# A banded attention with a gated feed-forward network: two last products behind the values, and a new written-out order

## The chip, the cores and the metric

The kernel runs on one core of one Trainium2 chip. The core has TensorE (PE, with its own queue of weight loads, PEld), VectorE (DVE), ScalarE (ACT), GpSimd (POOL) and SyncE (SP), which here only issues DMAs. Each engine runs its own instructions in the order of the program; semaphores hold an instruction back until another engine or a DMA is ready. The metric is the device time in microseconds (us), median of the runs. The kernel before took 745.35 us (three runs, 744.77 to 746.07).

## The reference

```python
def _attn_ref(q_l, k_l, v_l, q_g, k_g, v_g):          # 8 batches, 8 heads, 512 local and 32 global rows, width 64
    k_all = np.concatenate([k_g, k_l], axis=2); v_all = np.concatenate([v_g, v_l], axis=2)
    out_g = np.matmul(sm(scale * np.matmul(q_g, k_all.transpose(0, 1, 3, 2))), v_all)
    s_ll = np.where(np.abs(pos[:, None] - pos[None, :]) <= 32, scale * np.matmul(q_l, k_l.transpose(0, 1, 3, 2)), -1e9)
    s_lg = scale * np.matmul(q_l, k_g.transpose(0, 1, 3, 2))
    out_l = np.matmul(sm(np.concatenate([s_lg, s_ll], axis=-1)), v_all)
    return np.concatenate([out_g, out_l], axis=2)

def _moe_ref(x, w1, w2, w3, w_out):                    # x: 4352 rows of 512; d_ff is 1024
    return ((x @ w1) * (x @ w2)) @ w3 @ w_out
```

`sm` is a softmax over the last axis. The attention's output, heads side by side, is x of the second function.

## The kernel before, in words

The work is cut into some 3200 steps, each a few instructions of one engine. `PLAN` is a list of words such as `2479P`: step number 2479, on PE (A is ACT, D is DVE, V is POOL, S is SP). The list is the program's order: `list_schedule` only goes through it, and asserts that each step comes behind the steps it depends on (the lists that `add` is given). The instructions' semaphore waits follow from which tiles they read and write, in that order.

Attention runs over 32 pairs of heads, m = 0 to 31 (four per batch). For a pair: `scores` (step sp_m, 64 short matmuls, L431), on DVE the row maxima and on ACT the exponentials, sum, normalisation, two transposes on DVE (L457, L460), eight copies called moves (L474) on ACT, DVE and POOL, then `values` (step av_m, L485 to L496, 84 short matmuls). Scores and values take turns in a PSUM ring of two buffers named "pu".

The feed-forward part runs on split numbers, high and low halves, three matmuls for one product. `first` and `second` serve batches 0 and 1. From batch 2 on, `batch_seven` computes the gate products in seven instead of eight block products. For batch b and output column j = 0 to 7 the step m_b_j_ph (`seven`, L876) has four phases: phases 0 to 2 are 12 matmuls of 256 columns, phase 3, called the last product here, is 6. Columns 2q and 2q+1 are a column pair; it runs beside attention pair m = 4b + 4 + q, that is the next batch's. The even column uses PSUM banks "a" and "b", the odd column a buffer of the ring "pu" (tiles named j). After the last product DVE makes the gate product g1 (L902), and only then may the next column pair, or the next scores, take the bank again. Other steps of a column: cc and c2 (copies on ACT), a0 and b1 (DVE, L894 and L892), b0 and g0 (POOL or DVE). `second` (second_k_i, L638 to L640, 6 matmuls of 512 columns) multiplies by the folded weights.

SP issues the weight loads wl_b_q_x (512 KB each, L806, x = A0, A1, C0, C1, D, B0, B1) into a ring of seven buffers; each load waits until the products of the weights seven places before it are done: B1 of column pair q+1 waits for the last product of the odd column, B0 for that of the even column, D for phase 2 of both.

Of the kernel before, what the change touches and what calls it, by code (L numbers as in the profile page):

```python
# [31 lines left out]
def r(ap):  # L32
# [120 lines left out]
    1004D 1013A 1014D 1016D 1006D 1005A 2050S 1008D 1015A 1017A 1007A 1018D 2112P 1077D 1010D 1019A 1011A 1009A 2051S
    1020D 1021D 1040A 2109P 2110P 2052S 2116A 1023D 2126A 2123P 2127A 1022D 425S 2117D 1029A 1028D 2053S 1027D 1026V
    1030A 1031A 2128D 2113P 1038S 2124P 1024A 2054S 1025A 2119D 1032P 2118D 1033A 2120D 2114P 2129D 2125P 2130D 2131D
    1034A 1036V 2121D 2133V 998V 2132D 2056S 2137P 1035D 2141A 2055S 2134D 1041P 1050D 1042D 2138P 1051A 2135P 1044D
    1046D 1043A 2148P 1045A 1052D 2057S 1054D 1047A 2187V 1056D 1053A 2136P 2058S 1055A 1048D 1049A 1057A 2189D 2142A
    1058D 1059D 1864S 1061D 2152A 2149P 2139P 1060D 1113S 2153A 1064A 1067D 1066A 1062A 1068D 426S 1069D 1076S 1063A
    2150P 1065D 1070P 2143D 2195A 2145D 2219A 2155D 960V 2197A 427S 2154D 1151S 1078A 2199A 2144D 1071A 2140P 2146V
    1072A 2156D 2220D 2157D 2198D 2147D 1866S 2159A 2224S 2167A 2200V 2151P 2158D 1079P 2160D 1073D 1189S 2221A 1115A  # L160
    2223S 2188V 1080D 2191V 2168V 2201A 1088D 1090D 2229S 2203A 1092D 1082D 2196V 1084D 1094D 1091A 1089A 2161P 1086D
    2162P 359P 2202D 2249P 2190D 299S 2217A 2226S 2163A 2171A 1083A 428S 1093A 2192V 2165D 2205A 2207A 2225S 2222V
    1085A 360D 2172D 366D 361A 2169P 2208V 1081A 362D 2194V 2170P 2175A 363D 2176D 2173P 367A 2193D 2230S 364S 2209A
    2174P 2228S 2211A 2260P 1095A 368D 1087A 1096D 2177P 2178P 2179A 2212V 302S 369D 2210V 2213A 2264A 2253A 2180D
    2181P 1097D 1098D 2206V 2204D 1116A 1114S 2164S 2218D 370S 1099D 1104A 2182P 2261P 2214D 1101V 1100A 2227S 1105D
    1102D 2215A 2265A 1107V 2250P 1106V 365S 371S 2254A 1103V 2255D 2262P 2216V 2231S 2267D 2251P 2256D 2263P 1108P
    2257D 2266D 2258D 1109A 2252P 2183D 2270D 1110A 2268D 2269D 1117P 2259D 1111D 2271A 1126D 1127A 1118D 1119A 1128D
    2275P 1120D 1129A 2279A 1121A 1130D 1131A 2286P 1122D 1153V 2290A 1132D 1124D 2232S 2276P 2233S 2287P 2272D 1123A
    2234S 1133A 2235S 1191D 1192V 1125A 1112V 1134D 2280A 2277P 1135D 1137D 1136D 2236S 1074V 2291A 2288P 2185A 2273P
    2166S 2293D 2289P 2292V 1145V 1144A 1143V 1141A 2237S 1152S 1227S 2294D 2238S 1139V 1140A 2243S 1142A 2240S 2282D  # L170
    2274P 2241S 2239S 1138V 2281V 2283D 2284V 2295V 1146P 2278P 2285D 2301P 1147A 1148A 1149D 1154V 2296D 1155P 1156D
    1157A 1158D 1159A 2242S 2244S 1164D 1165A 2297V 2298V 2312P 2316A 1160D 1162D 1161A 1166D 1168D 1169A 1167A 1170D
    1171A 1163A 1172D 2299P 2300P 2184S 429S 2186S 2245S 2313P 1190S 1173D 2305A 1228S 1229A 1230A 2302P 2246S 2247S
    1150V 2317A 2306A 2314P 2318V 430S 1174D 1175D 1181D 1179A 1178A 1180A 1183D 2303P 1176D 2248S 1177D 1182D 2308D
    1184P 2304P 2320D 2307D 2309D 2319D 2321D 2310D 2311D 2315P 1185A 2322D 1186A 2327P 2331A 1187D 2323V 2324V 2377V
    1193P 1202D 1194D 2338P 1196D 1198D 1203A 1195A 1204D 1188V 1197A 2328P 1199A 1206D 1265S 2325P 2326P 1208D 1205A
    1207A 1209A 1200D 1201A 2385A 2387A 2342A 1303S 1266S 2332A 1210D 2339P 1211D 1213D 2329P 2389A 1212D 2388V 2343A
    1219A 1221D 1218D 1220A 1215A 2340P 1217D 1341S 1216D 2344V 1214A 1222P 2335D 2333D 2336V 2346D 2347V 2334D 2349A
    2345D 2390D 2341P 2330P 2348D 2414S 1223A 1224A 1225D 2337D 2350V 2357A 1231P 2381V 2391A 2386V 2351P 2352P 2409A
    1232D 1240D 1234D 1241A 2358V 2413S 301S 1242D 1244D 1236D 1246D 431S 1238D 372P 2392D 2439P 2410V 2419S 2353A  # L180
    2378D 2361A 2415S 2380V 2355A 2416S 1247A 373D 2359P 2382D 1235A 374A 2362D 1239A 375D 376D 2360P 2363P 2418S 2407A
    1237A 2417S 2383V 1233A 2365V 2395A 377S 2364P 2411A 1243A 379D 2366D 2397A 380A 2393A 1245A 2412D 2420S 381D 1248D
    2396D 2369V 2384V 2399A 2450P 382D 2367P 2370D 2379V 2401A 1267A 2400D 2398D 2368P 2454A 2371P 2372P 1268V 2394D
    1249D 2402V 2403A 432S 2443A 2404V 1250D 1251D 1252V 2440P 2451P 383S 1255D 2444A 378S 1254A 384S 2422S 1256A 2445D
    2455A 2405A 1253A 2441P 1257D 2421S 1259A 1379S 2423S 2452P 2354S 2456V 2446D 2447D 2448V 1258A 1260P 1261A 2406D
    2408D 1305A 2457D 2442P 2453P 2449D 1262D 2465P 2458D 2460D 2373A 1269P 2459D 1306D 1263D 2375A 2476P 2461V 1270D
    1278D 2469A 2424S 2466P 1304S 1271A 1279A 1280D 1272D 2426S 2425S 2462V 1274D 1276D 1282D 1273A 2427S 1281A 1284D
    2480A 1285A 1283A 1275A 2428S 1277A 2463P 1286D 1287D 1289D 2477P 1343A 1344V 2481A 2464P 1288D 1294V 1293V 2478P
# [80 lines left out]
def band_attention_glu_kernel(  # L269
# [22 lines left out]
    NP = H // 2  # L292
    PB = 1
    NF = PB * H
    NH = B * H
# [900 lines left out]
    def batch_seven(b):  # L1196
# [53 lines left out]
        for q in range(4):  # L1250
            for y in range(2):
# [163 lines left out]
    for b in range(NS, B):  # L1415
        batch_seven(b)
# [84 lines left out]
```

## Time and profile before

| what | value |
|---|---|
| median of 3 runs | 745.35 us (744.77 to 746.07) |
| the profiled execution's own time | 749.62 us |
| its span, first to last instruction | 747.7 us |
| PE busy | 720.7 us, 96% of the span |
| PEld, DVE, ACT, POOL busy | 84%, 66%, 52%, 30% |
| mean granted clock of TensorE | 0.993 |
| DMA | 176.60 MB, mean 236 GB/s; q1 holds the kernel's transfers, q8 and q14 are marked "instruction" (70 of 16 KB on q8: 1.15 MB) |

The page cuts the span into 40 slices; PE is at 9 tenths or more in nearly all of them. With an engine that full, the stretches in which it is not busy, and those in which it runs at a lower clock, are what is to be read. A wait view gives who waited for whom; "issue" stands where the engine waited for nothing that the profile shows. Weight loads (PEld) start ahead of their matmuls, so an idle stretch is read most sharply there.

### The profile page before, as it was taken

The numbers are of one execution on the slowest core, as the hardware profiler recorded it, in microseconds if no ns is written. First come the engines' busy times: TensorE is split into PE (matmuls) and PEld (weight loads), VectorE is DVE, ScalarE is ACT, GpSimd is POOL, SyncE is SP. The second block draws the span as 40 slices with busy tenths as digits, with TensorE's granted clock in tenths as the row PEclk, the third lists the DMA queues.
The fourth block names the chain that finished last, engine by engine and source line by source line (L and its number), as shares of the span: only waits on it lengthen the run. The fifth ranks groups of instructions, "written<-read, shape, count | busy, mean of one in ns | idle before, by whom it ended". The sixth has DMA issues, their size and how long they took to land.

```text
span 747.7 us, 22460 instructions
## 1 busy us (share of the span) xinstructions
PE 720.7 (96%) x8944; PEld 626.6 (84%) x8944; DVE 491.9 (66%) x1461; ACT 390.5 (52%) x1164; POOL 223.5 (30%) x334
## 2 busy tenths in 40 slices
PE   8999999999999999999999988999999999999994
PEld 5345788989989998889998977889988899899894
DVE  5999998885767765876568555856678667324211
ACT  3659986675455644754455634474555446222111
POOL 4013422342243332342244222333154143122100
PEclk9999999999999999999999999999999999999998
DMA  9786686687867897767974856677876685486740
GB/s 334 260 296 237 219 228 192 184 252 197 252 182 237 265 321 280 274 190 267 351 265 128 288 197 214 240 237 255 280 287 201 226 308 180 166 304 205 259 161 28
DMA packets 109091, 176.60 MB, mean 236 GB/s; under 512 B 11292, under 2 KB 57660, under 8 KB 108988
## 3 DMA queue, kind: packets, MB, share of 16 engines
q1 hardware_dynamic: 108988, 175.18, 71.1%
q8 instruction: 70, 1.15, 0.6%
q14 instruction: 33, 0.27, 0.1%
HBM read 144.97 MB, written 30.15 MB: 234 GB/s over the span
## 4 chain that ended last, share of the span: by engine, by line
PE 82%; DVE 6%; ACT 5%; DMA 3%; issue 2%; SPq 1%; ACTq 0%; DVEq 0%
PE j L876 15%; PE ap L876 14%; PE acc L638 8%; PE acc L640 8%; PE acc L639 8%; PE s L431 4%; PE av L485 4%; PE bp L605 2%; PE ap L605 2%; PE bp L606 2%; PE ap L606 2%; PE bp L607 2%; PE ap L607 2%; PE bp L876 2%; PE av L494 2%
## 5 line engine op out<-in xcount | busy, mean ns | idle before, releaser
L442 ACT ACTIVATE P<-P,small 128x128 f32<-128x128 f32 x256 | 99.9, 392 | 38.0 <-DVE small L436 37.8
L436 DVE CUSTOM_DVE_ANT_0 P<-s,cs 128x128 f32<-128x128 f32 x256 | 58.7, 286 | 36.8 <-PE s L431 35.7
L640 PE MATMUL acc<-w34h,gl 128*128 128x512 f32 x192 | 75.6, 394 | 0.0
L639 PE MATMUL acc<-w34l,gh 128*128 128x512 f32 x192 | 75.4, 393 | 0.0
L638 PE MATMUL acc<-w34h,gh 128*128 128x512 f32 x192 | 75.3, 392 | 0.0
L474 ACT COPY PT<-TT 32x256 f32<-32x256 f32 (+1 forms) x138 | 53.8, 390 | 14.8 <-DVE TT L457 10.0
L442 ACT ACTIVATION_READ_ACCUMULATOR P<-P,small 128x1 f32 x256 | 48.2, 188 | 0.0
L474 POOL COPY PT<-TT 32x256 f32<-32x256 f32 (+1 forms) x38 | 15.7, 413 | 106.0 <-DVE TT L457 92.4
L751 PE MATMUL w<-wo,w3f 128*128 128x512 f32 x96 | 44.1, 604 | 1.9 <-DVE wo L664 1.9
L431 PE MATMUL s<-KT,qp 64*32 64x128 f32 x2048 | 37.7, 274 | 6.3 <-issue 6.3
L640 PEld LDWEIGHTS acc<-w34h,gl 128*128 128x128 f32 x192 | 36.1, 188 | 7.4
L638 PEld LDWEIGHTS acc<-w34h,gh 128*128 128x128 f32 x192 | 36.1, 188 | 6.9 <-issue 0.8
L639 PEld LDWEIGHTS acc<-w34l,gh 128*128 128x128 f32 x192 | 36.1, 188 | 6.3
L452 DVE TENSOR_TENSOR P<-P,sums 128x1024 f32<-128x1024 f32 x32 | 39.9, 1248 | 0.8
L457 DVE STREAM_TRANSPOSE TT<-P 128x1024 f32<-128x1024 f32 x32 | 39.2, 1224 | 0.4
L431 PEld LDWEIGHTS s<-KT,qp 64*32 64x32 f32 x2048 | 28.7, 105 | 12.7 <-issue 7.7
L605 PE MATMUL ap<-x,w12h 128*128 128x256 f32 x128 | 36.1, 282 | 1.5 <-ACT as__1417 L611 0.8
L751 PEld LDWEIGHTS w<-wo,w3f 128*128 128x128 f32 x96 | 17.3, 190 | 22.9 <-issue 16.1
L888 POOL TENSOR_TENSOR bt<-bt 128x256 f32<-128x256 f32 x26 | 21.5, 829 | 50.3 <-ACT bt L890 49.9
L605 PE MATMUL bp<-x,w12h 128*128 128x256 f32 x128 | 36.2, 283 | 0.0
L607 PE MATMUL ap<-x,w12l 128*128 128x256 f32 x128 | 35.6, 278 | 0.2 <-DVE w12l L413 0.2
L485 PEld LDWEIGHTS av<-PT,vr 64*64 64x64 f32 x1024 | 28.5, 132 | 8.5 <-issue 4.3
(469 smaller groups left out, 2062.5 us busy)
## 6 DMA issues: line engine op xcount, KB each, us to landing
raw_w<-in_w_t_dram SPq DMA_DIRECT2D x22, 512.0 KB, 6.0
kq<-in_kp_t_dram SPq DMA_DIRECT2D x32, 272.0 KB, 5.4
out_dram<-o_None SPq DMA_DIRECT2D x33, 256.0 KB, 5.1
qp<-in_q_t_dram SPq DMA_DIRECT2D x32, 256.0 KB, 5.1
vr<-in_v_t_dram SPq DMA_DIRECT2D x32, 256.0 KB, 5.4
wg<-dm SPq DMA_DIRECT2D x16, 512.0 KB, 6.4
ws_0A<-dm SPq DMA_DIRECT2D x12, 512.0 KB, 5.3
ws_0C<-dm SPq DMA_DIRECT2D x12, 512.0 KB, 5.9
```

The costliest lines, as they stand in the source:

```text
L431: nc.tensor.matmul(st[32 * a : 32 * a + 32, x, 128 * e : 128 * e + 128], q[r, 128 * e + 32 * a : 128 * e + 32 * a + 32], k[r, o : o + 128] ...
L436: nc.vector.tensor_tensor_reduce(Ps[m % 2][:, x, e], T["s", m][:, x, 128 * e : 128 * e + 128], masks[e], -0.125, 3.0e38, ALU.add, ALU.min, ...
L442: nc.scalar.activation(p, p, AF.Exp, bias=T["mn", n][:, e : e + 1], scale=-1.0, accum_out=T["sm", m][:, x, e : e + 1])
L474: (nc.scalar.copy if eng is nc.scalar else eng.tensor_copy)(dst, src)
L485: nc.tensor.matmul(av[c, y, 128 * k + 32 * s0 : 128 * k + 32 * s1], V[r, x, k], PT[r, s0:s1, x, k], start=(k == 0), stop=False, **go)
L605: nc.tensor.matmul(d, wh, x[:, 0, 0:w], start=(k == m % 2 == 0), stop=False, skip_group_check=True)
L607: nc.tensor.matmul(d, wl, x[:, 0, 0:w], start=False, stop=(k == 3), skip_group_check=True)
L638: nc.tensor.matmul(a, gh[:, m % 2, sl], wh[:, c], start=(m == 0), stop=False, **part)
L639: nc.tensor.matmul(a, gh[:, m % 2, sl], wl[:, c], start=False, stop=False, **part)
L640: nc.tensor.matmul(a, gl[:, m % 2, sl], wh[:, c], start=False, stop=(m in (5, 7)), **part)
L751: nc.tensor.matmul(T["w34", t], w3f_of(t, j), wo_of(j), start=(j == 0), stop=(j == 7))
L876: nc.tensor.matmul(d, w[:, n, wy, kt, :], v[:, xy, :], start=(start and kt == c == 0), stop=(kt == 1 and c == 2), skip_group_check=True)
```

## The change

One line of the dependence lists, and the words of `PLAN` from its 1109th on. The line is in `batch_seven`; it made the last product of an even column (y == 0) depend on the values of its attention pair, and now does so for both columns:

```diff
-                    mid = [("av", NP * b + NP + q)] if ph == 3 and y == 0 and NP * b + NP + q < NH // 2 - 1 else []
+                    mid = [("av", NP * b + NP + q)] if ph == 3 and NP * b + NP + q < NH // 2 - 1 else []
```

In `PLAN` the first 1108 words are the same (up to the moves of pair 11), and so are the 524 words from second_8_6 behind the scores of pair 24 to the normalisation of pair 29. In the rest the words stand in another order, and 185 steps are on another engine (51 from DVE to POOL, 46 back, 33 from ACT to DVE, 23 back, 19 from POOL to ACT, 13 back). No step is added or removed. Two lines of it around the scores of pair 22 (1307P; 1298P is av_21, 2479P m_4_3_3, 2468P m_4_2_3, 2433S and 2431S the loads wl_4_2_B1 and wl_4_2_D, 433S the load of pair 22's v):

```diff
-    2470A 1290A 1297A 2430S 1291A 2484D 2483D 2467P 1295D 1296A 1292D 2479P 1298P 2472D 2473D 2471D 2482V 2374S 1299A
-    2486D 2468P 2475D 2485V 2474V 1300A 2487V 1301D 1307P 2429S 1316D 1308D 2491P 1309A 1310D 2431S 433S 2433S 1312D
...
+    1298P 1299A 2484D 2482V 2485D 2479P 2433S 2431S 1300A 2474V 2486D 2468P 1301D 1307P 2487V 1308D 2488V 433S 2502P
```

What stands on PE between the values of a pair and the next scores, where it differs (PE's order, read out of the two lists):

```
             before                          after
av_15        m_2_6_3 m_2_7_3                 m_2_6_3 m_2_7_3 second_4_6              sp_16
av_16        m_3_0_3                         m_3_1_3 m_3_0_3                         sp_17
av_17        m_3_2_3 m_3_4_0                 m_3_3_3 m_3_2_3 m_3_4_0                 sp_18
av_21        m_4_2_3                         m_4_3_3 m_4_2_3                         sp_22
av_22        m_4_4_3                         m_4_5_3 m_4_4_3 second_8_3              sp_23
av_30        m_6_4_3                         m_6_4_2 m_6_5_3 m_6_4_3                 sp_31
```

The list now has both last products behind the values in all 19 column pairs that the line names; before, it had so in 14 (that of pair 15 among them), and in those of pairs 16, 17, 21, 22 and 30 one of the two stood ahead of the values. SP's order around the scores of pairs 21, 22 and 23 (parts of its list):

```
21 before  wl_4_1_C1 store_6_0 wl_4_1_D load_q2_22 wl_4_1_B1 wl_4_1_B0
   after   wl_4_1_C1 store_7_0 wl_4_1_B0 wl_4_1_D wl_4_1_B1 load_q2_24
22 before  wl_4_2_C0 wl_4_2_D load_v_22 wl_4_2_B1 wl_4_3_A1 wl_4_2_B0
   after   wl_4_2_C1 store_6_128 wl_4_2_B1 wl_4_2_D load_v_22 wl_4_2_B0
23 before  wl_4_3_C0 load_v_23 wl_4_3_D load_k2_26 load_q2_24
   after   wl_4_3_C0 wl_4_3_A0 load_k2_25 wl_4_3_C1 wl_5_0_A0
```

On DVE, column pair 4, 5 of batch 2: before, b1_2_5, a0_2_5, g0_2_5, g1_2_4, with a0_2_5 behind m_2_5_3 in the list; after, a0_2_5 ahead of the values, then b1_2_4, b1_2_5, g1_2_4, with g1_2_4 ahead of m_2_5_3. At the end the first of the two last half evictions (out_16_128_0) goes from ACT to DVE.

## Rows read from the trace of the kernel before

**Rows 1.** Windows view by stage; columns: stretch, length, busy time (count) of PE, PEld, DVE...
```profile
236.00:477.57 241.57, 232.06 (x3208) 211.38 (x3191) 162.14 (x501) 128.38 (x405) 80.38 (x118) 0.99 0.75 253
477.57:590.00 112.43, 111.23 (x1433) 99.49 (x1428) 80.02 (x263) 60.87 (x194) 36.66 (x54) 1.00 0.74 252
590.00:738.30 148.30, 147.52 (x1358) 136.52 (x1358) 57.56 (x148) 45.41 (x116) 34.33 (x50) 1.00 0.62 210
```

**Rows 2.** Waits of the weight-load queue (PEld), 236 to 477.5; total, times, longest.
```profile
PEld s L431 <- issue: 6.2, 3, 2.8
...
PEld j L876 <- DVE cc L894: 1.0, 1, 1.0
PEld s L431 <- ACT gh L410: 1.0, 1, 1.0
```

**Rows 3.** Timeline at pair 22's scores, 435 to 439 (start, length, count, idle before).
```profile
434.94 0.81 PEld L431 LDWEIGHTS s<-KT,qp 64*32 64x32 f32 x54
...
438.56 0.17 PEld L431 LDWEIGHTS s<-KT,qp 64*32 64x32 f32 x10 [2.82 <-issue]
```

**Rows 4.** Timeline of PEld at pair 23's scores, 456 to 460.
```profile
459.88 0.14 PEld L431 LDWEIGHTS s<-KT,qp 64*32 64x32 f32 x2 [2.60 <-issue]
```

**Rows 5.** Windows view from gap to gap, and of the run-up to the second gap.
```profile
420.69:438.55 17.86, 15.21 (x252) 13.92 (x252) 9.43 (x31) 7.47 (x26) 5.99 (x10) 1.00 0.73 253
438.55:459.87 21.32, 18.13 (x252) 16.66 (x252) 11.11 (x34) 7.77 (x27) 3.82 (x6) 0.92 0.72 239
...
432.36:435.70 3.34, 3.34 (x139) 3.17 (x132) 1.55 (x5) 0.70 (x2) 2.49 (x3) 1.00 1.01 361
454.10:457.25 3.15, 3.15 (x138) 2.98 (x132) 1.74 (x4) 0.21 (x1) 1.90 (x2) 1.00 1.01 358
```

**Rows 6.** DMA view, 432.4 to 436.1: queue, kind, packets, MB, share of engines.
```profile
q1 hardware_dynamic: 541, 1.27, 95.1%
q14 instruction: 1, 0.01, 0.5%
```

**Rows 7.** DMA view, 436.1 to 438.6.
```profile
q8 instruction: 1, 0.02, 2.4%
```

**Rows 8.** DMA view, 438.6 to 441, GB/s in 40 equal slices.
```profile
GB/s 0 0 0 0 0 0 0 0 0 0 0 0 0 0 0 0 0 0 0 0 0 273 0 0 0 0 0 0 0 0 0 0 0 0 0 0 0 0 0 0
```

**Rows 9.** Timeline of SP's DMA issues, 404 to 482.
```profile
430.53 0.53 SPq L806 DMA_DIRECT2D ws_2D<-dm  x1
431.11 0.59 SPq L393 DMA_DIRECT2D vr<-in_v_t_dram  x1
431.89 0.32 SPq L806 DMA_DIRECT2D ws_2B<-dm  x1
```

**Rows 10.** Windows view of the two stretches at the lower clock (last columns: PEclk, DMA).
```profile
439.70:443.12 3.42, 3.42 (x18) 3.42 (x17) 1.49 (x13) 2.38 (x12) 0.00 (x0) 0.50 0.02 5
460.18:463.60 3.42, 3.42 (x17) 3.39 (x17) 2.54 (x18) 2.79 (x13) 0.00 (x0) 0.50 0.03 10
```

**Rows 11.** Timeline, 288 to 300: the wait before the first product of column 6.
```profile
294.92 0.42 DVE L894 TENSOR_TENSOR cc<-j,cc 128x256 f32<-128x256 f32 x1 [3.23 <-PE j L876]
...
296.24 1.61 PE L876 MATMUL ap<-x,ws_3A 128*128 128x256 f32 x12 [1.36 <-issue]
```

**Rows 12.** Timeline of PE, 448 to 466: the last product of column 5.
```profile
452.66 0.97 PE L876 MATMUL j<-x,ws_2B 128*128 128x256 f32 x6 [0.85 <-DVE cc L894]
```

**Rows 13.** The chain in order of time: scores 13, a product, values 13.
```profile
264.41 1.09 PE s L431 x64
...
273.93 1.36 PE j L876 x12
275.29 0.98 PE av L485 x30
```

**Rows 14.** Timeline of VectorE, 416 to 440: pair 21 from scores to values.
```profile
421.67 0.29 DVE L436 CUSTOM_DVE_ANT_0 P<-s,cs 128x128 f32<-128x128 f32 x1
...
430.71 1.09 DVE L474 COPY PT<-TT 32x256 f32<-32x256 f32 x2
```

**Rows 15.** Timeline of PE, 355 to 360: a bank taken again at once.
```profile
357.88 1.63 PE L876 MATMUL ap<-x,ws_2A 128*128 128x256 f32 x12 [0.52 <-DVE G1l L902]
```

**Rows 16.** Timeline of the end, 734 to 748.
```profile
738.30 0.65 ACT L645 COPY o<-acc 128x256 f32<-128x256 f32 x2 [0.77 <-PE acc L640]
```

More of the change, by code (lines that the diff above doesn't have):

```diff
@@ L250 @@
[L250 removed]
+    913V 912D 914A 300S 911A 1846P 2031S 917D 1995D 1976D 1978S 349D 916A 354A 1822S 1831P 1832P 1839A 885V 848V 350D
+    355D 1840D 1983D 1820S 351S 1847A 1848D 1901S 1984V 1997V 2032S 1977S 1985A 1986D 297S 2033S 1988S 927P 352S 1841P
+    1842P 356D 357S 1855P 1853P 2034S 2035S 2007A 2008V 1996D 1849A 1854P 1856P 1987S 928D 930D 931A 929A 932D 933A
+    2028V 1998V 934D 935A 936D 938D 939A 1850V 1851P 1852P 940D 942D 919A 920A 921D 1999D 2009A 2029A 2001D 2010D 1989D
@@ new lines @@
+    967A 981A 969A 1075S 2045S 2083P 979A 970D 971A 972D 425S 973A 982D 983D 985D 2100A 2086P 2047S 2084P 984D 2090A
+    2097P 2101A 2048S 2087P 986A 988D 993D 990D 987D 989D 2093D 992A 991A 2098P 2104D 1993S 2102V 994P 2092D 2103D
+    1039V 2088P 2105V 995D 2099P 2095D 2106D 2091V 2094D 1002A 2111P 996A 997D 2050S 1003P 2051S 1004D 2107A 2049S
+    2115A 1012D 1014D 2057S 2108V 1038S 2122P 1016D 1018D 1006D 1013A 1008D 1015A 998V 1017A 1010D 1005A 2109P 2052S
+    1007A 2110P 2053S 1011A 1009A 1019A 1020D 2126A 2112P 1021D 2123P 2116A 2117V 960V 2054S 2127A 1023D 2113P 1022D
@@ new lines @@
+    1062A 2144D 1070P 2159A 2140P 299S 1071A 2160D 2151P 2147D 2219A 1072A 2200V 1073D 2161P 2189V 2158D 2221A 2191D
+    2196D 2188D 1079P 1088D 2201A 2203A 2162P 1080D 2229S 2167A 1115A 2217A 1081A 2224S 2202V 1090D 2249P 428S 1082D
+    1092D 1084D 2192V 1094D 1083A 2171A 2163A 1086D 2222D 359P 2165A 2168D 1085A 2220D 2230S 2190D 360D 2169P 2205A
+    2194V 361A 2207A 2172D 362D 2208V 363D 366D 2209A 2193V 1093A 2210D 364S 1087A 2170P 1089A 2175A 367A 2228S 2173P
+    2176D 2174P 368D 2179A 1095A 2164S 1114S 369D 1091A 1096D 2211A 2260P 2180D 2177P 2213A 1097D 1116A 2204V 2178P
@@ new lines @@
+    2264A 2215A 370S 2206D 2181P 2182P 2227S 365S 2253A 2261P 1099D 1098D 2265A 2214V 1103A 2212D 2183D 1106A 371S
+    2250P 2262P 1107A 1101D 2254A 2251P 1104A 1102V 922V 2267D 2268D 1100A 1105A 2255D 2232S 1108P 2218D 2216D 2231S
+    2263P 2256D 2266V 2257D 1109A 1110A 1112V 2252P 2270D 2259D 1117P 2275P 2258V 1111D 1126D 1118D 1128D 2269V 1127A
+    2286P 1120D 1129A 1121A 1122D 1124D 2279A 2276P 1125A 1119A 1074V 2290A 2233S 2287P 2185D 1130D 1132D 1131A 1123A
+    2271V 2234S 1153V 2272D 2280A 1133A 302S 2235S 2277P 1191D 1192V 2291A 1134D 1135D 1137D 1136D 2236S 2288P 2273P
@@ new lines @@
+    1357A 2517P 1348D 435S 1358D 2528P 1360D 1350D 2515P 2521A 1361A 1349A 2567V 1351A 1359A 1352D 1353A 2569V 1362D
+    2518P 1363D 2532A 1365D 2575A 2522A 1364D 1368D 1371D 2529P 1367D 2519P 1370D 2533A 1373D 303S 2523D 1369A 1366A
+    2530P 1372A 2577A 2579A 2604S 1374P 1493S 1375A 2606S 436S 2536D 2599A 2524D 2520P 2535D 2531P 2580V 2568D 2525D
+    2376S 2534V 1376D 2526V 2527D 2547A 1377D 2601A 2537V 2571D 2581A 2538D 2576D 2516P 2539A 2540D 1383P 1384D 304S
+    2541P 2578D 2542P 2600V 1392D 1386D 1394D 1396D 1388D 1398D 1390D 2573V 2548D 2607S 2582D 2572D 2543A 2545A 2605S
@@ new lines @@
+    1264V 385P 386D 2551V 2552D 387A 2570D 388D 2608S 2602V 2574V 389D 392D 1457A 1458A 2629P 2610S 1418S 2549P 2550P
+    2555V 2556D 393A 394D 390S 2585A 2587A 2588V 2583A 2584V 2589A 2590V 2586V 1395A 1397A 1385A 1393A 1389A 2553P
+    1302V 2554P 2557P 2558P 2609S 306S 2544S 395D 396S 391S 397S 1226V 2597A 2598V 2640P 2611S 2546S 305S 2633A 2630P
+    2612S 1391A 1387A 1399A 1400D 2644A 2641P 2559A 2560D 2561P 1401D 2562P 2591A 2593A 2594D 2592D 1402D 1403D 1409D
+    2645A 1410D 2642P 1405D 2634A 2635D 2613S 2631P 1406D 2595A 2646V 1419A 1456S 2614S 2637D 2636D 1408A 1407A 1411A
@@ new lines @@
+    2790V 2743P 407D 1539A 2791A 2744P 2830P 2792V 2745A 2760D 2746D 1549A 2764D 2775A 1646S 2777A 2779A 2749V 2781A
+    440S 2783A 1543A 2774V 2785A 1551A 2747P 408D 1572D 2778V 2787A 2750D 1537A 2748P 2784V 2834A 2782D 2751P 409S
+    1552D 2823A 2776D 2752P 2780D 1553D 1555D 2820P 2824A 2786V 1554D 1556D 1560D 2825D 404S 1559D 410S 2831P 1563A
+    2835A 1562V 1561V 2821P 1558V 2832P 2826D 1557D 2827D 1564P 2837D 2788V 2822P 2753A 2836D 2838D 2839D 2828D 2829D
+    2841A 2842D 2833P 2840D 2734S 2755D 2800S 2845P 2849A 2736S 1573P 2802S 2846P 2801S 1378V 1565D 1566A 1609V 2806S
@@ L251 @@
+    3198P 3192V 3193P 3200D 3201A 3202D 3134S 3194P 3203P 3204P 3205P 3206P 3209A 3207P 3208P 3211D 3210S 3213A 3212S
+    3214S
 """.split()
```

182 lines of the change are left out of this document (74 added, 108 removed).

## The prediction

> **What bounds the kernel now.** Read the windows view by stage first. TensorE is busy 232.06 of 241.57 us in the first rewritten stretch, 111.23 of 112.43 in the stretch whose order is unchanged, 147.52 of 148.30 in the last [rows 1]. So PE sets the time, and only PE's idle time and its slower clock can be won: no step leaves PE. The first stretch idles 9.5 us, the other two 2.0 together. There the change must earn.
>
> Second, the waits of the weight queue in that stretch: 6.2 us in three waits stand at the scores (L431) with "issue", that is, for nothing that the profile shows [rows 2]. The timeline shows what they look like: pair 22's scores run 54 of 64 weight loads, then nothing for 2.82 us, then the rest [rows 3]; pair 23's stop for 2.60 us with two to go [rows 4]; the third is the remainder, 6.2 - 2.82 - 2.60 = 0.8. A semaphore would hold scores at their start, not in the middle. Third, the windows from gap to gap: from the first (420.69) to the second (438.55) PE takes 252 weight loads and 252 matmuls, and from the second to the third (459.87) 252 and 252 again [rows 5]. With some 8 semaphore instructions, which I add as an estimate, that is 512 both times. Gaps that recur at a fixed count of instructions point to the instruction stream. Fourth, the DMA view: from 432.4 to 436.1 the kernel's own queue q1 moves 541 packets at 95.1% of the engines and q8 none [rows 6]; in 436.1 to 438.6 one q8 packet marked "instruction" comes [rows 7], and then PE goes on. My reading: PE gets its instructions in blocks of 256 (16 KB of 64 bytes, if one packet is one block). A block is asked for when the one before it begins. It waits behind loads that SP issued: 1.25 MB in 430.5 to 432.2 [rows 9].
>
> Three things follow. Count 256 instructions back from the second gap: the block begins at 432.36, and its run-up takes 3.34 us (values, one last product, scores: 132 weight loads, some over the edges); before the third gap it is 3.15 us [rows 5]. The fetch took from 432.36 to about 436.15 to start (3.8) and from there to 438.56 to arrive (2.4): 6.2 us, against 3.34. With an empty queue the next one started at 439.86 (the one busy slice), 1.3 us after its predecessor block began at 438.56 [rows 8]: 1.3 + 2.4 = 3.7 us. So a block of 256 that lasts under 3.7 us stalls always, one over 6.2 us hardly, and between them SP's loads decide.
>
> [...]
>
> [...]
>
> **The change, part by part.** Sum against the profiled execution's 749.62 us (span 747.7, 1.9 around it).
>
> The new dependence itself adds no semaphore; the list is only checked against it. What it forces is five odd or even last products behind their values.
>
> *Gaps at the scores.* At pair 22 one more last product (12 instructions, 0.68 us, half of a 12-matmul phase's 1.36 [rows 13]) takes the place of 12 mean ones (3.34 / 256 x 12 = 0.16): the block lasts 3.34 + 0.52 = 3.9 us. At pair 23 a last product and a second (6 x 512 columns, as many as a phase: 1.36 us) come in: 3.15 + 0.68 + 1.36 - 0.3 = 4.9. Pair 21's block is as before. Bounds: with the fetch as late as now, 2.3 + 1.3 + 0.8 = 4.4 us stay; with an empty queue (3.7) none. Which end? At pair 22 SP's list now has B1, which waits for the odd last product, ahead of D and of load_v_22. All three thus issue behind the values, 2 us after the block begins, where now they were issued in the 2 us before it and made the 3.8. At pair 21, B0 (which waits for a product behind the values) now stands ahead of D and B1, with the same effect. At pair 23 two or three loads are still issued just ahead. I take 0.6 us left, near the lower end: 5.6 of 6.2 gone.
>
> *Clock.* With gaps of at most 1 us no fall: 2 x 1.7 = 3.4 gone; nothing gone if a gap over 2.6 stays.
>
> *Semaphore waits.* Three of now have an answer in the new list. The first product of column 6 (batch 2) waited 1.36 us, because on DVE a0 of column 5 stood ahead of g1 of column 4 and waited for the last product of column 5 [rows 11]; a0 now stands earlier. Pair 16's scores waited 1.0 us [rows 2] for the buffer of column 7; second_4_6 (1.36) now stands between. The last product of column 5 (batch 4) waited 0.85 us for DVE [rows 12]; pair 22's values, whose L485 part alone takes 0.98 us in pair 13 [rows 13], now cover it. Together 3.2. A wait that stays: column 4's bank taken again at once, 0.52 us [rows 15]. New ones: scores behind the odd last product now need its g1; the even last product (0.68) covers what cost 0.52 with nothing between, so 0 to 5 x 0.52 = 2.6 us. And 185 steps on other engines will be late somewhere: the unchanged stretch idles 1.20 us in 112 [rows 1], which over the 390 rewritten us makes 4.2; today's two stretches, without the gaps, have 9.5 - 6.2 + 0.8 = 4.1. So between -3.2 (only the names count) and +2.6 (only the new covers); I take -1.2, nearer to the rate, which says 0.
>
> *Cover of the softmax.* From scores to values PE has now 9.8 us of other work in most columns: 265.5 to 275.29 in pair 13, with no wait [rows 13]. In pairs 21, 22 and 30 it shrinks to that, by a last product (0.68) or by one and a phase or second (2.0). Pair 21's first maximum began at 421.67 and its last move ended at 431.80 [rows 14], 10.1 us, so its moves must end 0.5 us earlier; pair 13 shows that they can. Cost 0; to 0.5 us a column if not.
>
> *SP's loads.* Ring and release order are the same; a load still follows the products seven places back. *End.* One half eviction on DVE beside ACT's: -0.65 to 0 us [rows 16], taken as 0.
>
> Sum: -5.6 - 3.4 - 1.2 = -10.2 us: 739.4 for the profiled execution. The median of the runs is 4.27 below it (749.62 - 745.35). If those 4.27 lie outside the terms, the median becomes 745.35 - 10.2 = 735.2; if they all lie in gaps and clock (the late fetch may be later under the profiler), the gain is 5.9 and it is 739.4. I take the middle: **737 us**, own range 735 to 739.5.
>
> **Rivals.**
> 1. *The fetch stays as late as now.* 4.4 us of gaps stay and one fall of the clock (1.7): gain 9.6 - 6.1 + 1.2 = 4.7, 740.7 us. For it: DMA is busy at 0.75 in this stretch [rows 1]. Against: SP's order at pairs 21 and 22.
> 2. *The gaps don't go.* Either they aren't fetches, or blocks fall on fast runs elsewhere (the counts are shifted by the new order) with the same 6.2 + 3.4: only 1.2 is won, 744.2 us. Against: the two large gaps stand at two of the five column pairs in which a last product moves. For: every run of values and scores is a candidate.
> 3. *Slower: the values wait for their moves.* In nine columns (pairs 13, 14, 15, 18, 19, 21, 22, 23, 30) the new list leaves 9.8 us for the softmax. If DVE's new order makes each late by the longest wait of this stage, 1.36 us [rows 11], that is 12.2: 745.35 - 10.2 + 12.2 = 747.4. It decides from (10.2 + 1.5) / 9 = 1.3 us a column. Against: pair 13 ran with 9.8 without a wait, and VectorE is busy only 162 of 242 us [rows 1].
>
> **How the numbers follow.** Forecast 0.58, rival 1 0.22, rival 2 0.12, rival 3 0.08. A measurement here tells 0.2% (1.5 us) from no change. Forecast and rival 1 are faster by more, and so is a sixth of rival 2: 0.82; the rest of it is the same: 0.10; slower 0.08. The range runs from 733 (all three waits gone, none new) to 744, just short of rival 2.
>
> **What would show it.** The windows view: PE idle in the first stretch at 3 to 5 us instead of 9.5. The waits at L431 with "issue" under 1.5 us instead of 6.2; PEclk 1.00 throughout the stage. The DMA view: the q8 packet in pair 22's values, not behind them. In the timeline no 1.36 us ahead of batch 2's column 6. Wrong would be: a gap over 2 us in the middle of scores, a clock of 0.50 in the stage, or values that wait for moves (L474) in several columns.

## The result, and the profile after

The changed kernel takes 739.65 us (median of five runs, 735.87 to 741.75). The kernel before, run beside it, took 745.35; the ratio is 0.9906, with a 95% interval of 0.988 to 0.9932. It is faster by 5.7 us. The forecast was 737 in a range of 733 to 744. The profiled execution after took 739.65 us (span 737.8), that of before 749.62 (747.7): 9.97 less.

The windows view by stage comes first, as in [rows 1]: stretch, length, busy time (count) of PE, PEld, DVE, ACT and POOL, PEclk, DMA share, GB/s.

```profile
237.30:466.89 229.59, 227.24 (x3208) 207.35 (x3191) 161.54 (x509) 126.21 (x398) 80.64 (x118) 1.00 0.80 268
466.89:579.00 112.11, 111.26 (x1433) 99.43 (x1428) 79.92 (x263) 60.88 (x194) 36.45 (x54) 1.00 0.74 248
579.00:728.50 149.50, 147.10 (x1359) 136.23 (x1358) 54.57 (x146) 47.12 (x119) 37.99 (x50) 1.00 0.61 210
```

The first rewritten stretch lost 12.0 us (241.57 - 229.59): its idle time went from 9.51 to 2.35, its PE busy time from 232.06 to 227.24 for the same 3208 matmuls. The stretch with the old order is 0.3 shorter, the last one 1.2 longer. Where the last windows are cut moves work between them by a few tenths; by steps (table below) the part behind second_8_6 is 0.8 us longer, and the beginning, whose order did not change, 1.3.

The waits of the weight queue in that stretch answer to [rows 2] (total, times, longest):

```profile
PEld ap L877 <- ACT bt L891: 2.0, 1, 2.0
...
PEld s L432 <- issue: 1.1, 3, 0.4
```

The 6.2 us at the scores with "issue" are 1.1, none over 0.4. A wait of 2.0 us is new. TensorE's own waits in the stretch, before (first fence, 240 to 480) and after (all that the view has, 236 to 466.9), show what of this was idle time of PE itself: no wait at the scores is left there.

```profile
PE s L431 <- issue: 6.3, 4, 2.6
PE ap L876 <- issue: 1.4, 1, 1.4
PE j L876 <- DVE cc L894: 0.8, 1, 0.8
...
```

```profile
PE ap L877 <- ACT bt L891: 1.8, 1, 1.8
PE ap L877 <- DVE G1l L903: 0.5, 1, 0.5
```

The scores of pairs 22 and 23, where [rows 3, 4] had gaps of 2.82 and 2.60 us, now run through (PEld's timeline: start, length, count, idle before):

```profile
434.17 0.89 PEld L432 LDWEIGHTS s<-KT,qp 64*32 64x32 f32 x64
...
449.95 0.89 PEld L432 LDWEIGHTS s<-KT,qp 64*32 64x32 f32 x64 [0.36 <-issue]
```

Why the fetch comes in time at pair 22 is seen in the DMA view of 432.2 to 434.9, from the end of the values to the last of the scores (queue, kind: packets, MB, share), and in SP's timeline:

```profile
q1 hardware_dynamic: 46, 0.12, 20.0%
q8 instruction: 1, 0.02, 2.2%
```

```profile
433.59 0.32 SPq L807 DMA_DIRECT2D ws_2B<-dm  x1
433.96 0.53 SPq L807 DMA_DIRECT2D ws_2D<-dm  x1
434.54 0.59 SPq L394 DMA_DIRECT2D vr<-in_v_t_dram  x1
```

In [rows 6] q1 had 541 packets at 95.1% in the like stretch and q8 none. Now B1 waits for its buffer until 433.59 and holds D and the load of v behind it on SP ([rows 9]: D 430.53, v 431.11), so the queue is nearly empty when PE's next block is fetched: the q8 packet comes between 432.3 and 432.6, while the last weight loads of the values run.

What is new and bad is in two rows of PE's timeline and three of ACT's:

```profile
411.77 0.96 PE L877 MATMUL ap<-x,ws_0D 128*128 128x256 f32 x6 [1.83 <-ACT bt L891]
...
604.49 0.97 PE L877 MATMUL ap<-x,ws_2B 128*128 128x256 f32 x6 [1.38 <-DVE cc L893]
```

```profile
406.54 0.59 ACT L646 COPY o_None<-acc 128x512 f32<-128x512 f32 x1
410.64 0.59 ACT L646 COPY o_None<-acc 128x512 f32<-128x512 f32 x1 [3.51 <-DMA out_dram<-o_None]
411.13 0.59 ACT L891 COPY bt<-ap 128x512 f32<-128x512 f32 x1
```

On ACT the copy c2_4_0 (411.13) stands behind the second half of the eviction out_7, and that waits 3.51 us for the store of an earlier output to free its buffer. Phase 2 of column 0 of batch 4, m_4_0_2, waits for the copy. The wait at 604.49 is the last product of column 4 of batch 6: DVE has a0_6_5 in front of b1_6_4, and a0_6_5, behind m_6_5_3 in the list, starts only when that product is done.

### The profile page after: what moved, and what is told of

Same layout as the page of the kernel before. It is cut to its first block, busy times and chain, and to the rows that moved or that the text cites. A ratio compares the mean times of both kernels' runs of the same rounds, so it can differ in the third digit from the quotient of the medians.

```text
span 737.8 us, 22464 instructions
## 1 busy us (share of the span) xinstructions
PE 716.0 (97%) x8944; PEld 623.1 (84%) x8944; DVE 489.3 (66%) x1467; ACT 389.9 (53%) x1159; POOL 226.6 (31%) x333
## 4 chain that ended last, share of the span: by engine, by line
PE 81%; DVE 8%; ACT 4%; DMA 4%; issue 1%; SPq 0%; DVEq 0%; ACTq 0%
PE j L877 16%; PE ap L877 13%; PE acc L639 8%; PE acc L641 8%; PE acc L640 7%; PE s L432 4%; PE av L486 4%; PE bp L877 2%; PE bp L606 2%; PE ap L606 2%; PE bp L607 2%; PE bp L608 2%; PE ap L607 2%; PE ap L608 2%; ACT P L443 2%; PE av L495 2%
## 5 line engine op out<-in xcount | busy, mean ns | idle before, releaser
L897 POOL TENSOR_TENSOR bt<-cc,bt 128x256 f32<-128x256 f32 x29 | 21.4, 745 | 65.7 <-DVE cc L895 54.0
L606 PE MATMUL ap<-x,w12h 128*128 128x256 f32 x128 | 36.1, 282 | 1.6 <-ACT as__1417 L612 0.8
L608 PE MATMUL bp<-x,w12l 128*128 128x256 f32 x128 | 35.6, 278 | 0.0
L607 PE MATMUL ap<-x,w12h 128*128 128x256 f32 x128 | 35.6, 278 | 0.0
```

The lines of the kernel that those rows point to most:

```text
L606: nc.tensor.matmul(d, wh, x[:, 0, 0:w], start=(k == m % 2 == 0), stop=False, skip_group_check=True)
L607: nc.tensor.matmul(d, wh, x[:, 1, 0:w], start=False, stop=False, skip_group_check=True)
L608: nc.tensor.matmul(d, wl, x[:, 0, 0:w], start=False, stop=(k == 3), skip_group_check=True)
```

## The experiments

The table has a stage for every kernel: from the values ahead of pair 12's scores to second_8_6 (the middle, 233.57 to 477.57 before), and from there to the start of PE's last but one matmul (the end). Length and PE busy time of the middle are one row of the windows view each; the low clock is the number of stretches at 0.50 in it. Each ratio is to the runs of the kernel before beside that kernel; their medians were 745.35 beside after, 745.59 beside e1 to e4, 746.29 beside e5 to e8 and 744.92 beside e9 to e11.

| kernel | median us | ratio to before, 95% | middle, PE busy | low clock | end |
|---|---|---|---|---|---|
| before | 745.35 | 1 | 244.00, 234.49 | 2 | 260.31 |
| after | 739.65 | 0.988 to 0.9932 | 232.03, 229.68 | 0 | 261.14 |
| after, run again (e11) | 739.18 | 0.9886 to 0.9935 | 234.46, 231.67 | 1 | 260.56 |
| before + 160 PE instructions (e1) | 745.77 | 0.9982 to 1.0026 | 234.41, 230.17 | 0 | 260.47 |
| after + 160 (e6) | 747.07 | 0.9989 to 1.004 | 233.41, 230.48 | 0 | 262.88 |
| before + 64 (e7) | 753.38 | 1.0074 to 1.0152 | 241.84, 232.82 | 1 | 262.25 |
| after + 64 (e4) | 752.33 | 1.0063 to 1.0108 | 239.03, 232.79 | 1 | 263.39 |
| before, PE's order (e2) | 741.74 | 0.9929 to 0.9965 | 237.48, 230.59 | 0 | 258.63 |
| before, SP's order (e3) | 740.59 | 0.9909 to 0.9951 | 238.86, 232.58 | 1 | 259.08 |
| before, both (e10) | 740.34 | 0.9903 to 0.9953 | 235.78, 231.06 | 0 | 258.70 |
| after, SP undone (e8) | 742.97 | 0.9939 to 0.9978 | 234.71, 231.76 | 1 | 260.78 |
| after, five moves (e5) | 735.34 | 0.9832 to 0.9891 | 231.64, 229.88 | 0 | 258.59 |
| after, seven moves (e9) | 732.93 | 0.9803 to 0.9856 | 229.48, 229.48 | 0 | 257.28 |

The stages are those of one profile each. They differ by more than the edits do: e2, e3 and e10 leave the order of the end as it was before, and it is 1.2 to 1.7 us shorter there.

**Where the blocks end.** The idle products at the start of the kernel are made more, by narrow ones of 16 columns; each is two weight loads and two matmuls (9024 matmuls instead of 8944 with 40). They shift every later instruction against the borders of the blocks and change nothing else of the order.

```diff
-IDLE = {None: ((0, 128, 256),) * 13}
+IDLE = {None: ((0, 128, 256),) * 13 + ((0, 128, 16, 32),) * 40}     # 160 PE instructions; 16 for 64 of them
```

> The kernel before, with 40 more idle products (16 columns, 160 PE instructions) at the very start; PE's later order, the loads and all other engines as before. Theory A (PE's instructions come in blocks of 256, and a block that runs shorter than its fetch takes leaves a gap): block ends lie 160 instructions earlier in the work, so the gaps inside the scores of pairs 21, 22 and 23 (0.8, 2.8, 2.6 us) go, and so do the two stretches at clock 0.50; the shortest blocks of the stage (4.0 us) now end in the scores of pair 20 and, in the unchanged stretch, of pair 26, with gaps of 0 to 2.2 us there. PE idle from pair 12's scores to second_8_6 falls by 4 to 8 us from 9.5, the start costs 2 to 5 us more. Rival B (the gaps come from semaphores or from the order of the other engines): that order is the same, so the gaps at pairs 22 and 23 stay at 2.6 to 2.8 us and the clock falls behind them.

> The changed kernel, with 16 more idle products (64 PE instructions) at the start. Theory A: the changed order is good for its own phase of the blocks only; 64 instructions earlier the short blocks are those that end in the scores of pair 17 (3.8 us) and of pair 30 (3.9) and in the joined values and scores of pairs 11 and 12 (2.6), so gaps of 0 to 2.4 us come back there, 1 to 3.6 at pair 12; time 2 to 8 us over the changed kernel, of which 1 to 2 at the start. Rival E (both last products behind the values are cover enough wherever the blocks fall): no gap over 0.5 us inside scores, time within 2 us of the changed kernel.

The kernel before with 160 more has no gap at pairs 21 to 23 and no low clock in the middle, 9.6 us less there; its idle time fell from 9.51 to 4.24, within the 4 to 8 expected. Rival B is out. But the whole is no faster: the start took 3.7 us more (the middle began at 237.29 instead of 233.57), 2.5 of it for the idle products (their weight loads end at 11.60 instead of 9.12), with a gap of 3.21 us in the scores of the first pairs, another gap (1.4) came in the unchanged stretch, and the median is 745.77. The profile is 5.9 us shorter than before's (743.76 against 749.62) and the median is not: the profiled execution of before was an unusually long one, as the next section shows. The changed kernel with 64 more is 12.7 us slower than without, not the 2 to 8 expected, and slower than the kernel before: gaps stand at other scores, and behind the one at 346.58 the clock is 0.50. PEld's timeline of the first and of the second run, and the windows view of the second:

```profile
16.51 0.17 PEld L431 LDWEIGHTS s<-KT,qp 64*32 64x32 f32 x11 [3.21 <-issue]
```

```profile
346.58 0.14 PEld L431 LDWEIGHTS s<-KT,qp 64*32 64x32 f32 x2 [2.37 <-issue]
...
600.77 0.16 PEld L431 LDWEIGHTS s<-KT,qp 64*32 64x32 f32 x8 [2.11 <-issue]
```

```profile
348.00:350.00 2.00, 2.00 (x11) 2.00 (x11) 2.00 (x11) 1.28 (x6) 0.00 (x0) 0.50 0.33 121
```

So the gaps hang on the count of instructions. Then the same two shifts for the other kernel each (PEld's timeline of e7):

> The changed kernel with 40 more idle products ahead of the first one (160 more PE instructions), as the earlier run did with the kernel before. Theory A (the gaps depend on which instruction of PE a block of the program ends at; the order itself is worth the waits it removes less those it adds): at this place of the borders neither order has a gap between 235 and 470 us, so the middle stage is 2 to 3 us shorter than the 234.4 us of the kernel before with the same 40 products, 231.5 to 232.5, and the whole 2 to 4 us below that kernel (738 to 743.5 where the idle products cost some 3 us at the start). Rival B (the order as such is worth the 5.7 us): 739 or below, and the middle stage 228 to 230.

> The kernel before with 16 more idle products ahead of the first one (64 more PE instructions), as the earlier run did with the changed kernel (752.3 there). Theory A: the borders of the blocks fall into the same scores as in that run, but the kernel before has less work between the values and the next scores of pairs 22 and 23, and 30 and 31, so that gaps of 1 to 2.6 us come there as well as near 61, 344 and 600 us: 753 to 759, a middle stage of 241 to 246 us. Rival B (the shift cost the changed kernel something that its own order has): no dearer than the kernel before, 744 to 748.

```profile
350.13 2.64 PEld L876 LDWEIGHTS ap<-x,ws_1A 128*128 128x128 f32 x12 [2.63 <-issue]
...
463.31 0.57 PEld L431 LDWEIGHTS s<-KT,qp 64*32 64x32 f32 x34 [2.25 <-issue]
...
603.00 0.17 PEld L431 LDWEIGHTS s<-KT,qp 64*32 64x32 f32 x10 [1.69 <-issue]
```

The row of 463.31 shows the count at its clearest. Before, pair 23's scores stopped with two weight loads to go [rows 4]; with 64 instructions (32 weight loads and 32 matmuls) more at the start they stop with 34 to go. In both the windows view from 0 to the end of the gap counts 11823 weight loads and matmuls. The other gaps stand whole blocks away from there: by the 252 of [rows 5], those at 350.13 and 603.00 in e7 are 11.98 blocks ahead and 15.02 behind (8804 and 15608), those at 346.58 and 600.77 in e4 12.00 and 15.04 (8800 and 15612), that at 518.12 in e1 7.02 behind (13592).

The kernel before with 64 more (rows above, PEld) has its gaps beside the same steps as the changed one, and a larger one at pair 23 (2.25 instead of 0.86 there): the middle is 2.8 us dearer, as expected. The other expectation missed: with 160 more the changed kernel should have been 2 to 4 us below the kernel before and is 1.3 above. Its middle is only 1.0 shorter, its end 2.4 longer and its start 2.1 (239.35 against 237.29). Part of the start is the clock: behind the first pairs' gap it is 0.91 from 20 to 22 us in e6 (gap 3.34) and 1.00 in e1 (3.21). So at equal shift the new order gives -5.7 us (none), -1.05 (64; 752.33 - 753.38) and +1.3 (160; 747.07 - 745.77). The runs of these two pairs stood beside different runs of the kernel before; by their ratios it is 1.0086 against 1.0113 and 1.0014 against 1.0004, that is -2.0 and +0.7 us, and both pairs of intervals overlap. At two of three shifts, then, no gain clear of the noise is left. What the changed kernel wins it owes mostly to where its instructions stand against the borders and the loads; what its order as such is worth, these runs do not settle.

**The three gaps taken apart.** First PE's part of the change around pairs 21 to 23, then one swap in SP's order, each in the kernel before. The first puts m_4_3_3 behind av_21, m_4_5_3 behind av_22 and second_8_3 behind m_4_4_3:

```diff
-2479P 1298P ... 2490P ... 2505P ... 1336P ... 2494P
+1298P 2479P ... 1336P 2505P ... 2494P 2490P
```

> The kernel before, with three PE steps moved as in the change and nothing else: m_4_3_3 behind the values of pair 21, m_4_5_3 behind those of pair 22, second_8_3 behind m_4_4_3. Theory A: the block before pair 22's scores lasts 3.9 us instead of 3.4 and that before pair 23's 4.9 instead of 3.2; with the fetch as late as before (6.2 and 5.8 us) the gaps are 2.3 and 0.9 us, with an empty queue none. At most one stretch at clock 0.50. Gain 2 to 8 us. Rival C (only SP's order of loads decides): both gaps stay over 2.5 us and the time stays within 1 us of before.

The second puts wl_4_2_B0 ahead of wl_4_2_D:

```diff
-2431S 433S 2433S ... 2432S
+2432S 2431S 433S 2433S
```

> The kernel before, with one load moved on SP: wl_4_2_B0, which waits for a product behind pair 22's predecessor's values, stands ahead of wl_4_2_D, load_v_22 and wl_4_2_B1, so that these three are issued behind the values and not in the 2 us before the fetch. PE's order is as before. Theory A with the queue as cause of the delay: the fetch starts 1.3 to 1.5 us after its predecessor block began instead of 3.8, the gap in pair 22's scores falls from 2.8 to 0.3-0.6 us and no clock of 0.50 follows it; pair 23's gap stays near 2.6 with its fall of the clock. Gain about 4 us. Rival D (the number of PE instructions between values and scores alone decides, whatever the queue): the gap at pair 22 stays 2.8 us.

With PE's order (first fence) the gaps of pairs 21 and 23 are 1.31 and 1.29 us, that of 22 is 0.57, and the clock stays up. With SP's order (second fence, PEld, and third, DMA of 430.5 to 434.3) those of 21 and 22 are gone, that of 23 stays with its low clock. So rivals C and D are both out. The gap of pair 21 must not be counted for either edit: both stand behind it in the lists, and it was 0.77 us before, 1.31 with PE's order and none with SP's. By so much a gap differs from one execution to the next.

```profile
421.31 0.40 PEld L430 LDWEIGHTS s<-KT,qp 64*32 64x32 f32 x30 [1.31 <-issue]
...
455.48 0.13 PEld L430 LDWEIGHTS s<-KT,qp 64*32 64x32 f32 x2 [1.29 <-issue]
```

```profile
433.61 0.89 PEld L430 LDWEIGHTS s<-KT,qp 64*32 64x32 f32 x64
...
453.89 0.14 PEld L430 LDWEIGHTS s<-KT,qp 64*32 64x32 f32 x2 [2.52 <-issue]
```

```profile
q1 hardware_dynamic: 71, 0.23, 14.6%
q8 instruction: 1, 0.02, 1.8%
```

A swap of one load thus gives 0.993 of the time of before: the run-up in instructions was unchanged, only the queue was nearly empty.

> The kernel before with the two earlier edits together: wl_4_2_B0 ahead of wl_4_2_D in SP's order, and on PE m_4_3_3 behind the values of pair 21, m_4_5_3 behind those of pair 22, second_8_3 behind m_4_4_3. Alone they gave 740.59 and 741.74. Theory A (each takes away part of the same three fetch gaps: SP's order those of pairs 21 and 22, PE's order all that made the third one fall to the low clock and 1.2 us of it): no gap over 1.4 us in pairs 21 to 23 and no stretch at clock 0.50; middle stage 235 to 236.5 us, 738.5 to 740.5. If they add up in full (5.0 + 3.8): 736.8. Rival (one edit moves SP's loads back in front of the other's fetch): 741 to 744 with a gap over 1.5 us.

Together they give 740.34, the time of the whole change with four words moved, and no more than one of them alone: each takes what the other would. It came out within the expectation; no wait over 0.5 us with "issue" is left for the weight queue at the scores.

**SP's order undone in the changed kernel.** The loads wl_4_2_D and load_v_22 go ahead of wl_4_2_B1 again.

```diff
-2433S 2431S ... 433S
+2431S 433S 2433S
```

> The changed kernel with one thing undone in SP's order: the loads wl_4_2_D and load_v_22 ahead of wl_4_2_B1 again, as in the kernel before (in the changed kernel they stand behind it, and it waits for its buffer until 433.6 us, after the scores of pair 22 are all but done). Theory A (the block that PE needs at the end of those scores is fetched late when SP's loads are in the DMA engines at that time): a gap of 1 to 2.6 us comes back near 435 us, alone or with a stretch at clock 0.50 behind it that takes 1.7 us more; 741 to 744 in all. Rival (the loads have no part in it; the run-up in products sets the gap): no gap there, and the time of the changed kernel, 738.5 to 740.5.

The DMA view, 432.3 to 435.6 and then 435.6 to 436.5, PEld's timeline, and the windows view of another place:

```profile
q1 hardware_dynamic: 493, 1.14, 94.6%
...
q8 instruction: 1, 0.02, 7.0%
```

```profile
438.06 0.16 PEld L430 LDWEIGHTS s<-KT,qp 64*32 64x32 f32 x9 [0.82 <-issue]
```

```profile
414.00:416.00 2.00, 2.00 (x11) 2.00 (x11) 0.42 (x1) 0.00 (x0) 0.53 (x1) 0.50 0.99 384
```

The picture of [rows 6, 7] is back: 493 packets at 94.6% and no q8, which comes behind them, and the scores stop. With e3, where the opposite swap took pair 22's gap away, that shows the cause there. The size missed: 0.82 us, less than the 1 to 2.6 expected, and the low clock in this run follows the wait of m_4_0_2, not this gap. The median, 742.97, is 3.3 to 3.8 us above the changed kernel's, and the profile accounts for 0.8 of it (the middle is within 0.3 of the second run of the changed kernel, which has the same low stretch; the middle began 1.9 us later). The rest stays open.

**The new waits.** Five entries of the changed kernel's order are moved:

```diff
-2373A ... 2375A ... 2444A        # c2_4_0 behind out_7
+2444A 2373A ... 2375A
-2889D 2885P 2890D                # a0_6_5 behind m_6_5_3
+2889D 2890D 2885P
-2647D 2639D ... 2648D            # a0_5_1 behind g1_5_0
+2647D 2648D 2639D
-2850A ... 2860A                  # cc_6_3 behind c2_6_2
+2860A 2850A
-2289P ... 2278P                  # m_3_2_3 behind m_3_3_3
+2278P 2289P
```

> The changed kernel with five entries of its order moved, none of which changes the count of PE instructions ahead of a later step: c2_4_0 (ACT) ahead of the eviction out_7_0, a0_6_5 (DVE) ahead of m_6_5_3, a0_5_1 (DVE) ahead of g1_5_0, cc_6_3 (ACT) ahead of c2_6_2, m_3_2_3 (PE) ahead of m_3_3_3. In the trace of the changed kernel these five places cost 2.0, 1.5, 1.1, 1.1 and 0.7 us over the usual duration of the step; with the moves 2.0, 1.4, 0.8, 0.5 and 0.4 of it should go. Theory A (what is left in the changed kernel is these waits, and the fetch stays ahead as the block borders stand where they did): 4 to 5 us below the changed kernel, 734.5 to 736, no gap over 1.2 us left between 120 us and the end. Rival (a product that comes earlier takes cover from an instruction fetch, and a gap with its low clock comes back): some of the 5 us is spent in a gap of 1 to 2.6 us and a stretch at clock 0.50, 737 to 741.

735.34: the end lost 2.5 us, the waits at a0_6_5 and a0_5_1 are gone, and no gap over 0.8 us came back. That the end would have no gap over 1.2 us held, but in the middle one stayed: two moves failed. The one on cc_6_3 changed nothing, since that product waits for a weight load ("0.93, DMA ws_1C" in PE's timeline). And out_7's wait came back one product later: c2_4_1 stands behind it too. ACT's and PE's timeline:

```profile
408.50 0.59 ACT L644 COPY o_None<-acc 128x512 f32<-128x512 f32 x1 [1.12 <-DMA out_dram<-o_None]
...
409.84 0.59 ACT L889 COPY bt<-j 128x512 f32<-128x512 f32 x1
```

```profile
410.48 0.97 PE L875 MATMUL j<-x,ws_0D 128*128 128x256 f32 x6 [1.50 <-ACT bt L889]
```

So the eviction goes behind c2_4_1, and the load that PE waits for goes ahead of the one that blocks it on SP:

```diff
-2373A ... 2375A ... 2455A        # out_7 ahead of c2_4_1
+2455A 2373A 2375A
-2806S ... 2803S                  # wl_6_1_C1 behind wl_6_1_B1
+2803S 2806S
```

> The run with five moves, with two things more. Its trace shows that c2_4_0's wait came back one product later: c2_4_1 (ACT, 409.84) still stands behind the second half of the eviction out_7, which waits 1.12 us for the store of an earlier output, and m_4_1_2's phase starts 1.9 us after the one before. So out_7_0 and out_7_128 now stand behind c2_4_1. And the load wl_6_1_C1 stands ahead of wl_6_1_B1 in SP's order: it stood behind loads whose buffer comes free at 567.8, and PE waited 0.93 us for it at 577. Theory A (these are the last two waits of about a microsecond behind 235 us, and the fetch stays ahead): 1.5 to 2.6 us below the five moves (735.34), 732.7 to 734, a middle stage of 229.8 to 230.3 us instead of 231.65. Rival (the eviction is needed by the next user of its bank, or the values of pair 20 come earlier and the scores of pair 21 to 23 run into a fetch): one of them takes the gain back, 735 to 738, with a gap over 0.8 us between 408 and 450.

732.93 us, below both kernels (interval 0.9803 to 0.9856 of before; the changed kernel beside it, below, has 0.9886 to 0.9935). The windows view of the middle and the end:

```profile
233.89:463.37 229.48, 229.48 (x3310) 209.94 (x3309) 163.34 (x512) 127.18 (x400) 81.28 (x118) 1.00 0.82 272
463.37:720.65 257.28, 257.28 (x2790) 235.53 (x2785) 134.22 (x407) 108.02 (x313) 74.61 (x104) 1.00 0.68 230
```

PE's busy time equals the length in both: between 234 and 721 us this view has no idle time left. The middle is a little under the 229.8 to 230.3 expected.

> The changed kernel as it is, beside the other two on the same chip, as the measure for them: 738 to 741 us; 0.6% to 1.1% below the kernel before.

739.18, within 0.5 us of the first time. But its middle is 2.4 us longer, by one thing: the wait of m_4_0_2, which in the first profile left the clock alone, is followed by the low clock here (timeline of PE, then windows):

```profile
411.17 1.26 PE L877 MATMUL ap<-x,ws_0D 128*128 128x256 f32 x6 [2.09 <-ACT bt L891]
```

```profile
412.00:415.00 3.00, 3.00 (x16) 3.00 (x15) 0.42 (x1) 0.45 (x1) 0.95 (x2) 0.50 0.96 353
```

## Why the prediction was right, and where it was not

*What bounds it.* Right: all of the gain came from the first rewritten stretch. e9, with no idle time left there in the view, needs 229.5 us for the same instructions.

*Gaps, -5.6.* Right in size and place: 6.2 became 1.1, in three waits of at most 0.4, so 5.1 are gone; in PE's own waits 6.3 became none. The cause is shown for pair 22: e3 takes its gap away by SP's order alone, e8 brings one back in the same way, with the q8 packet ahead of the loads in the one and behind 1.1 MB of them in the other. For pair 23 the run-up counts, by one profile each: there e3 leaves 2.52 us and e2, with a last product and a second more in the run-up, 1.29 and no low clock. Pair 21's gap went as well, but it differs from one execution to the next without any change ahead of it.

*The block of 256.* Shown as a count: the gaps behind 240 us stand whole multiples of 252 weight loads and matmuls apart, under shifts of 0, 64 and 160; and the packed trace of before has on PE, in each of the two windows from gap to gap of [rows 5], 8 semaphore instructions beside the 252 weight loads and 252 matmuls, and two q8 packets of 16 KB. That is 512 instructions both times, as estimated; if both packets are PE's, it makes 256 a packet and 64 bytes an instruction. That a block is asked for when the one before it begins was the author's reading: no view has the request. The four packets of these windows begin 3.9, 3.8, 1.3 and 3.1 us behind a border; elsewhere in that trace, with the borders counted off by 256, some begin up to 3.4 us ahead of one. A late fetch costs: with 64 instructions more PE's weight queue stands for up to 2.4 and 2.6 us at a fetch, in either kernel, and in e8 for 0.8 behind the loads.

*Clock, -3.4.* Right that both stretches went in the first profile; the second (e11) has one, behind the wait of m_4_0_2, and a clock of 0.50 in the stage was among the signs of being wrong. The size was low: PE's busy time in the stretch fell by 4.8. No run shows the 1.7 us that the sum counts for a stretch, half of the 3.42 at 0.50 [rows 10]; in the changed kernel's two profiles, with the same order, one such stretch makes 231.67 - 229.68 = 2.0 us of PE busy time. The other 0.8 is not explained. No gap of at most 1 us is followed by a fall in any run (the longest of them is 0.99, in e7). The idle time ahead of a fall was 2.08 us or more, yet 3.13 us of idle ahead of the same product in e4 brought none: why it falls is not settled.

*Semaphore waits, -1.2.* Here the size missed. Outside the gaps PE's idle time in the three stretches was 5.2 us before (9.51 + 1.20 + 0.78 - 6.3) and is 5.6 after (2.35 + 0.85 + 2.40): 0.4 more. Of the three named, all went; column 6 of batch 2 now starts at 295.46 without idle. But pair 16's 1.0 us had been a wait of the weight queue alone, PE's waits have none there, so that the three were worth 2.2 and not 3.2. The new ones did not come from g1 behind the odd last products, as reckoned, but from an eviction that waits for a store (2.0 for the weight queue, 1.8 for PE) and from a0 behind its neighbour's product (1.4). Without gaps on either side, the new order's middle is 2.4 us shorter (234.41 in e1 against 232.03), 0.5 of which is a gap of e1's own; its end is 0.8 longer.

*Cover of the softmax, 0.* Right: one wait of values in the middle, 0.4 us for the weight queue and none for PE. So rival 3 did not come.

*From the profiled execution to the median.* Here the size failed. The sum was -10.2 and the profiled execution moved by -9.97; the median by -5.7. That the first two agree so well is partly luck: the gaps gave 6.3 and the clock 4.8, more than was put down, while the waits gave +0.4 and the beginning, which was not in the sum, +1.3. The prediction put the 4.27 us between the profile of before and its median half inside and half outside the terms ("I take the middle"); the lower end, 5.9, was the true one. The runs show part of why: of the 47 runs of the kernel before that stood beside the experiments, 742.34 to 751.76 us, one alone is longer than the profiled 749.62, so that profile had drawn nearly the worst. The nine with a mean granted clock of 0.991 have a median of 747.5, the 23 with 0.995 or more 744.8: the clock differs from run to run, and some 2.6 us go with it. The rest is not shown; the length of the gaps in runs without a profile is not seen. That the profiler itself makes the fetch later is not borne out: in the twelve other rows of the table the profiled execution lies between 2.0 us under the median and 2.2 over it.

*Rivals 1 and 2.* The median, 739.65, is nearer to rival 1 (740.7) than to 737, yet its mechanism did not come: no late fetch is left in the profile. It is the profile and not the time that tells the two apart. Rival 2's second form, blocks that end on fast runs elsewhere, did not happen here by the place where the counts fell, and does with 64 instructions more. The prediction followed the borders only through pairs 21 to 23, so that no other run of scores was hit is luck as far as its reasoning goes.

## What to carry to other kernels

Where PE stops in the middle of a run of short matmuls with "issue" and no semaphore, look at the instruction queue's packets: here the stops, the longest of 2.82 and 2.60 us, were late fetches, and they were moved by the count of instructions ahead and by loads that another engine issued just before. Before a new order is credited with such a gain, shift it: a few idle instructions at the start tell whether the order or its place against the blocks is what paid. And a wait has to be followed to its head: both large new waits stood behind an instruction that waited for something else.

## What the runs showed of the hardware

PE's late fetches behind 240 us stand at fixed counts of its instructions, whole multiples of 252 weight loads and matmuls apart to within 0.04 of a block. In the gaps of pairs 21, 22 and 23 before, PE went on 2.4, 2.4 and 2.6 us behind the q8 packet.

64 PE instructions at the start of either kernel cost 8.0 and 12.7 us of 740 to 745; the instructions themselves take 1.0 of it, an estimate from the 2.5 for 160 in e1, and the rest comes far behind them.

The same idle time ahead of m_4_0_2 was followed by a granted clock of 0.50 in two runs (first two rows, e8 and e11) and by none in three others (after, e6, e4; PEld's timeline), one of them with an idle time that is longer than all the rest:

```profile
412.43 0.77 PEld L875 LDWEIGHTS ap<-x,ws_0D 128*128 128x128 f32 x6 [2.08 <-ACT bt L889]
411.17 0.96 PEld L877 LDWEIGHTS ap<-x,ws_0D 128*128 128x128 f32 x6 [2.29 <-ACT bt L891]
411.77 0.77 PEld L877 LDWEIGHTS ap<-x,ws_0D 128*128 128x128 f32 x6 [2.03 <-ACT bt L891]
417.62 0.77 PEld L876 LDWEIGHTS ap<-x,ws_0D 128*128 128x128 f32 x6 [2.10 <-ACT bt L890]
420.68 0.77 PEld L876 LDWEIGHTS ap<-x,ws_0D 128*128 128x128 f32 x6 [3.13 <-ACT bt L890]
```
